# Three shifts in the order of issue of a fused attention and spectral-filter kernel

## The chip, the cores and the metric

The kernel runs on one core of one Trainium2 chip. The metric is the device time of one execution in microseconds. Times inside an execution are counted from the start of the span, which runs from the first to the last instruction of the profile.

The engines go by short names: PE is TensorE (its weight loads are shown as PEld), ACT is ScalarE, DVE is VectorE, POOL is GpSimd, SP is SyncE. Each takes its instructions in a fixed order of its own, and an instruction that waits holds up all that stand behind it on that engine. SP and POOL do little here but issue DMAs, and a row marked SPq or POOLq is such an issue.

## The reference

Two independent computations are put side by side in the output.

```python
# A: 16 query heads share one key head and one value head; S = 2048, D = 448, Dh = 28
q = (x @ wq) split into 16 heads;  k = x @ wk;  v = x @ wv
p = softmax(q k^T * Dh**-0.5);     a = (p v, heads joined) @ wo
# B: a filter in the frequency plane of a 2048 x 448 array
X = rfft2(x);  b = irfft2(X * (w_r + 1j * w_i))
out = concatenate([a, b], axis=-1)
```

## The kernel before

**First stage (about 0 to 69 us).** The queries and, folded into their spare rows, the keys and values are projected into `qraw`. The key and value rows are picked out of `qraw` by small DMAs (`fetch`, line 277) into `kf`: rows 0 to 31 are keys, rows 32 to 63 values. `fetch` takes row groups `ms`; groups 7 to 13 are value rows. The last two value groups, 12 and 13, for the last 512 positions, come out of the last projection and are fetched at line 479 through POOL. The value rows are then turned by 16 transposes on PE (line 509) and copied to `vs` (line 512). The queries of the first chunk are built at line 469. Each query is kept as two pieces, a high part `qh` and a low part `ql`, in four bands of 32 partitions of one tile, `qf`, for each of four heads; `copy_q` (line 207) writes one band of one head. Bands 2 and 3 are written by DMAs, band 2 by SP and band 3 by POOL (lines 486 and 487). Between these pieces of work the first transform of B is done (`fft1_...`), which stores its result in DRAM (`t1`). In this stage PE's order is the order of the program text, while the other engines' order is chosen by a scheduler; `behind(a, b)` only says that `a` is issued after `b` on their engine, with no wait.

**Main stage (about 69 us to the end).** There are 256 steps: 4 chunks of 512 queries, 4 groups of 4 heads, 16 blocks of 128 keys. A step makes four score products on PE (line 929), each into a PSUM bank of its own; their exponentials on ACT (line 864); and four value products (line 875) into one bank. There are eight banks, six named `s` and two (`sx`, `po`) that come from the first stage; one of the eight collects the value products and seven go round. `PLAN` (line 48) holds the steps in groups, each a string. `-` is a score whose exponential ACT takes straight from the bank. `k` is a score that DVE first copies out of its bank (line 935), with the exponential of a pair of copies made later at line 954. `e` is a score that ACT takes into the same kind of tile (line 940). Letters are units of other work on PE: `A` and `B` the two halves of the filter's middle stage, `W` a quarter or so of an output block (four `W` in a row finish one block of 128 rows), `Z` the filter's last stage. `spread` (line 38) makes the string; its fourth argument, `start`, sets how late the letters stand. Four `W` in a row are a `wo_unit` (line 799) for each of the four head groups.

DVE and ACT run in the order of the program text here. DVE's other work goes through a planner: `put` queues pieces of work with a cost, `passed(work)` moves PE's planned clock on after each product and takes pieces from the queue as long as DVE's planned clock isn't ahead of PE's, and `need` takes pieces until a given one is done. `at(step, f)` runs `f` when a step's scores are all issued.

**The middle stage's input.** `fft2_load(0)` (line 594) reads B's first result back from `t1` into the tile `b` with four DMAs on SP (line 599). `fft2_split(0)` (line 612) puts two pieces in the queue, a rounded copy `bh` (line 617) and the rest, written over `b` (line 618). `fft2_a(0)` (line 620) multiplies both on PE (lines 586 to 588). The first `A` stands in the group of steps 8 to 12, whose string is `-k-k-k-k----------A--`, at step 11.

**An output block's input.** `norm` puts the division and splitting of a head group's attention output in the queue; its last piece (line 772) is followed by small DMAs (`spares`, line 741) that bring some rows to spare partitions of `oh` (by SP, line 746) and `ol` (by POOL, line 749).

Of the kernel before, what the change touches and what calls it, by code (L numbers as in the profile page):

```python
# [20 lines left out]
S, D, H = 2048, 448, 16  # L21
# [16 lines left out]
def spread(n, units, lazy=4, start=0.9, rest=0.85, apart=1.0):  # L38

    late = 8 if lazy > 4 else 4  # L40
    m = 4 * n - late
    out = [(float(i), "-") for i in range(m)]
    out += [(apart * j + 0.5 if j < lazy else m + 0.1 * j, "k" if j < lazy else "e") for j in range(late)]
    out += [(m * (j + start) / (len(units) + rest) - 0.4, u) for j, u in enumerate(units)]
    return "".join(k for _, k in sorted(out)).replace("X", "WWWW").replace("Y", "ZZ")


PLAN = ["eeee"] + ["eeeeF"] + [spread(2, "", 0, 1.05)] + 2 * [spread(2, "", 0)] + [spread(5, "A", 4, 1.6)]
# [5 lines left out]
PLAN += [spread(6, "BAX", 4, 0.9, 0.85, 1.5)] + [spread(5, "BA", 4, 0.9, 0.6)]  # L54
PLAN += [spread(7, "BBX", 5, 0.9, 1.1)] + [spread(7, "ZZ", 8, 0.9, 0.85, 2.0)]
PLAN += [spread(7, "ZZZ", 6, 0.9, 0.48, 2.0)] + [spread(7, "ZZ", 8, 0.9, 0.6, 1.5)]
PLAN += [spread(7, "ZZZ", 6, 0.9, 0.6, 2.0)] + [spread(6, "X", 8, 0.9, 0.6, 2.0)]
PLAN += [spread(7, "X", 8, 0.6, 0.6, 1.5)] + [spread(8, "X", 8, 0.9, 0.6, 1.5)]
PLAN += [spread(7, "X", 8, 0.6, 0.35, 1.5)] + [spread(7, "ZZZ", 8, 0.9, 0.6, 1.5)]
PLAN += [spread(7, "Z", 8, 0.45, 0.6, 2.0)] + [spread(7, "ZZZ", 8, 0.9, 0.97, 2.5)]  # L60
# [12 lines left out]
def kernel(ctx: ExitStack, tc: tile.TileContext, t: dict):  # L73
    nc = tc.nc
# [21 lines left out]
    def behind(ins, other):  # L96

        tc.add_manual_dep(ins.ins, other.ins.name,
                          mybir.DependencyInfo(mybir.DependencyClass.NoSync, mybir.DependencyReason.DATA),
                          reason="order of issue")  # L100
# [65 lines left out]
    def fft1_b(q):  # L166
        return fft1_out(q, fft1_mm(q))
# [39 lines left out]
    def copy_q(i, p, q, src, eng):  # L207

        o, x = q[32 * p:32 * p + 32, i], src[32 * i:32 * i + 32].bitcast(F32)
        if eng is nc.scalar:  # L210
            return eng.activation(o, x, AF.Copy)
        if eng is nc.vector:
            return eng.tensor_copy(o, x)
        return eng.dma_start(o.bitcast(F32), x)

    def build_q(c, g, first=False):
        cs = slice(c * CW, (c + 1) * CW)
        qh = qp.tile([128, CW], F32R, name="qh", bufs=1)
        ql = qp.tile([128, CW], F32R, name="ql", bufs=1)
        qt = ql.bitcast(F32)  # L220
        if (c, g) not in qa:
            qa[c, g] = qp.tile([128, 4, CW], F32R, name="qa")
        q = qa[c, g]

        def split():
            nc.vector.tensor_tensor(ql, qt, qh.bitcast(F32), op=ALU.subtract)
            if first:
                return
            for i in range(4):
                for p, src in enumerate((qh, ql)):  # L230
                    mv = nc.sync.dma_start(q[32 * p:32 * p + 32, i].bitcast(F32), src[32 * i:32 * i + 32].bitcast(F32))
                    behind(mv, stored[-1])
            nc.sync.dma_start(q[64:128].bitcast(F32), q[0:64].bitcast(F32))

        def high():
            if first:
                return nc.scalar.activation(qh, qt, AF.Copy)
            return nc.vector.tensor_copy(qh, qt)

        ops = [(540, lambda: nc.vector.tensor_scalar(qt, qraw[:, g, cs], mask, cvec[:, g, c:c + 1],  # L240
                                                     op0=ALU.mult, op1=ALU.add)),
               (450, high), (710, split)]
        if not first:
            return ops
        for _, op in ops:
            op()
        return q, qh, ql
# [17 lines left out]
    with tc.tile_pool(name="w1", bufs=1) as w1:  # L265
# [11 lines left out]
        def fetch(ms, hs, eng=nc.sync):  # L277

            for m in ms:
                r, o = 32 * (m % 4) + DH, 32 * (m // 7) + 4 * (m % 7)  # L280
                last = eng.dma_start(kf[o:o + 4, hs], qraw[r:r + 4, m // 4, hs])
            return last
# [20 lines left out]
        with tc.tile_pool(name="x1", bufs=2) as x1:  # L303
# [127 lines left out]
            for c in range(1, NC):  # L431
                for g in range(NG):
# [25 lines left out]
                    if n in slots:  # L458
# [3 lines left out]
                        if n == 10:  # L462
# [6 lines left out]
                            qf, qh, ql = build_q(0, 0, True)  # L469
# [6 lines left out]
                            fft1_fold(q + 2, None if q < 3 else 0)  # L476
                        if q:
                            fft1_b(q - 1)
            fetch(range(12, 14), slice(1536, S), nc.gpsimd)


        behind(copy_q(0, 1, qf, ql, nc.scalar), last)
# [1 line left out]
            last = fft1_a_out(6, p, fft1_a_mm(6, p))  # L484
        for i in range(4):
            copy_q(i, 2, qf, qh, nc.sync)
            copy_q(i, 3, qf, ql, nc.gpsimd)
        behind(copy_q(1, 1, qf, ql, nc.scalar), last)
        top = terms(1, NC)
        for ins in fft1_fold(7, 1):  # L490
# [325 lines left out]
    def at(step, f, *a):  # L816
        later.setdefault(max(step, 0), []).append((f, a))
# [8 lines left out]
    where, total = {}, 0  # L826
# [6 lines left out]
        total += n  # L833
    fft2_consts()
    at(1, fft2_load, 0)
    at(where["A"][0] - 1, fft2_split, 0)
    at(where["B"][-1] + 1, fft3_consts)
    for u, step in enumerate(where["A"]):
        if u % 2 == 0 and u < 14:
# [66 lines left out]
    for tokens in PLAN:  # L906
# [10 lines left out]
        for k in tokens:  # L917
# [5 lines left out]
            i, h = divmod(x[kind], 4)  # L923
# [274 lines left out]
```

## Time and profile before

| | us |
|---|---|
| three timed runs | 633.93, 634.25, 634.91 |
| median of them | 634.25 |
| the profiled execution | 633.88 |
| its span | 632.1 |
| PE busy in the span | 626.7 (99%) |
| ACT busy | 547.3 (87%) |
| DVE busy | 440.2 (70%) |
| POOL busy | 61.5 (10%) |

In the rows of the timeline the first number is the start in the span, the second the duration, then engine, line, operation, tiles (out<-in), shape and count. A row can stand for several instructions of a kind in a row (x4). Brackets tell how long the engine was idle before it, and what ended that. Products on PE overlap, so that a start, not an end, tells how PE gets on: scores follow each other every 0.23 us where nothing holds them up.

### The profile page before, as it was taken

Reading aid. Unit: us, or ns where it says so; the run is one execution under the profiler, and the core shown is the slowest. Engines: PE = TensorE matmul, PEld = TensorE weight load, DVE = VectorE, ACT = ScalarE, POOL = GpSimd, SP = SyncE. Lnnn points to the kernel's source line nnn. Section 1 sums busy time; section 2 is a strip of 40 time slices with the busy share of each in tenths; the row PEclk is TensorE's granted clock in tenths of the full one; section 3 lists DMA queues with packets and bytes.
Section 4 is the critical chain, followed back from the end, with each engine's and each line's share of the span. In section 5 each row is a group of like instructions: output and inputs, shape, how many; then the busy total and the mean of one; then the engine's idle time right before and its main releaser. Section 6 shows DMA issues by size and latency. Waiting matters only on the chain. (4 is left out here: it accounts for less than half of the span.)

```text
span 632.1 us, 12164 instructions
## 1 busy us (share of the span) xinstructions
PE 626.7 (99%) x4436; PEld 377.6 (60%) x4436; DVE 440.2 (70%) x792; ACT 547.3 (87%) x985; POOL 61.5 (10%) x118
## 2 busy tenths in 40 slices
PE   9999999999999999999999999999999999999997
PEld 7877645656565655746555665565556565555555
DVE  5999648889998943867766845277687764457753
ACT  5655999999999998988889989999989989989991
POOL 3021401021212110000110100001010100000000
PEclk9999999999999999999999999999999999999999
DMA  8865973456455523226340413034152413030011
GB/s 260 285 175 165 271 161 92 111 147 184 117 153 123 147 58 74 69 64 187 77 108 16 125 36 82 16 83 148 37 127 60 104 51 90 16 82 13 19 31 61
DMA packets 37891, 66.74 MB, mean 106 GB/s; under 512 B 8009, under 2 KB 22746, under 8 KB 36860
## 3 DMA queue, kind: packets, MB, share of 16 engines
q1 hardware_dynamic: 32608, 52.50, 30.2%
q0 software_dynamic: 4640, 12.48, 7.9%
q8 instruction: 36, 0.59, 0.4%
q10 hardware_dynamic: 576, 0.92, 0.4%
q14 instruction: 31, 0.25, 0.1%
HBM read 29.81 MB, written 17.87 MB: 75 GB/s over the span
## 5 line engine op out<-in xcount | busy, mean ns | idle before, releaser
L864 ACT ACTIVATE p<-s 128x512 f32<-128x512 f32 x405 | 221.7, 635 | 26.8 <-PE s L929 26.1
L929 PE MATMUL s<-qa,ka 128*128 128x512 f32 x756 | 227.5, 402 | 0.0
L929 PEld LDWEIGHTS s<-qa,ka 128*128 128x128 f32 x756 | 138.2, 188 | 60.8 <-issue 26.8
L935 DVE COPY k<-s 128x512 f32<-128x512 f32 x122 | 80.1, 685 | 62.8 <-PE s L929 62.4
L875 PE MATMUL s<-p,vs 128*32 128x512 f32 x976 | 121.3, 595 | 0.0
L864 ACT ACTIVATE qraw<-s 128x512 f32<-128x512 f32 x137 | 79.0, 651 | 6.4 <-PE s L929 6.4
L954 ACT ACTIVATE k<-k 128x1024 f32<-128x1024 f32 x80 | 83.4, 1141 | 0.0
L875 PEld LDWEIGHTS s<-p,vs 128*32 128x32 f32 x976 | 29.4, 109 | 64.3 <-issue 59.4
L929 PE MATMUL sx<-qa,ka 128*128 128x512 f32 x137 | 55.2, 403 | 0.0
L929 PE MATMUL po<-qa,ka 128*128 128x512 f32 x131 | 53.0, 405 | 0.0
L864 ACT ACTIVATE p<-po 128x512 f32<-128x512 f32 x75 | 47.9, 639 | 4.5 <-PE po L929 4.2
L875 PE MATMUL s<-qraw,vs 128*32 128x512 f32 x384 | 49.5, 593 | 0.0
L864 ACT ACTIVATE p<-sx 128x512 f32<-128x512 f32 x64 | 41.2, 644 | 3.0 <-PE sx L929 2.9
L749 POOL DMA_DIRECT2D ol<-ol x36 | 18.0, 507 | 227.4 <-DVE ol L772 155.3
L875 PE MATMUL s<-k,vs 128*32 128x512 f32 x304 | 39.7, 594 | 0.0
L929 PEld LDWEIGHTS sx<-qa,ka 128*128 128x128 f32 x137 | 25.8, 188 | 11.0 <-issue 4.2
L929 PEld LDWEIGHTS po<-qa,ka 128*128 128x128 f32 x131 | 24.6, 188 | 11.0 <-issue 5.0
L879 DVE STREAM_TRANSPOSE osb<-s 128x512 f32<-128x512 f32 x13 | 9.3, 716 | 27.7 <-PE s L875 27.6
L875 PEld LDWEIGHTS s<-qraw,vs 128*32 128x32 f32 x384 | 12.0, 110 | 27.3 <-issue 26.1
L935 DVE COPY k<-po 128x512 f32<-128x512 f32 x17 | 11.7, 685 | 21.4 <-PE po L929 21.3
L864 ACT ACTIVATE qraw<-sx 128x512 f32<-128x512 f32 x35 | 22.7, 649 | 2.0 <-PE sx L929 2.0
L935 DVE COPY p<-s 128x512 f32<-128x512 f32 x35 | 23.0, 682 | 0.0
(278 smaller groups left out, 972.7 us busy)
## 6 DMA issues: line engine op xcount, KB each, us to landing
qa<-qa SPq DMA_DIRECT2D x15, 512.0 KB
raw<-xa SPq DMA_DIRECT2D x16, 256.0 KB
xb<-xb SPq DMA_DIRECT2D x8, 512.0 KB
qa<-qh SPq DMA_DIRECT2D x64, 64.0 KB
qa<-ql SPq DMA_DIRECT2D x60, 64.0 KB
t<-bs SPq DMA_DIRECT2D x16, 225.0 KB
wr<-wr POOLq DMA_DIRECT2D x16, 225.0 KB, 4.0
wi<-wi POOLq DMA_DIRECT2D x16, 225.0 KB, 5.4
```

The costliest lines, as they stand in the source:

```text
L749: nc.gpsimd.dma_start(ol[c][o, g].bitcast(F32), ol[c][r, 0].bitcast(F32))
L864: nc.scalar.activation(tiles[-1][:, h % 2], sc, AF.Exp, scale=SCALE)
L875: mm(po[c, g][32 * i:32 * i + 32], vs[:, kc], ps[i // 2][:, i % 2], start=(n == 1), stop=(n == 16))
L879: nc.vector.transpose(o, po[c, g])
L929: begun.append(mm(sc, ka[:, kc * 128:(kc + 1) * 128], qa[c, g][:, h], start=True, stop=True))
L935: nc.vector.tensor_copy(keep[i][h // 2][:, h % 2], sc)
L954: nc.scalar.activation(p, p, AF.Exp, scale=SCALE)
```

## The change

Three places change, and none adds or removes an instruction.

```diff
-PLAN += [spread(7, "ZZZ", 6, 0.9, 0.6, 2.0)] + [spread(6, "X", 8, 0.9, 0.6, 2.0)]
+PLAN += [spread(7, "ZZZ", 6, 0.9, 0.6, 2.0)] + [spread(6, "X", 8, 1.15, 0.6, 2.0)]
...
-            fetch(range(12, 14), slice(1536, S), nc.gpsimd)
+            fetched = fetch(range(12, 14), slice(1536, S), nc.gpsimd)
...
         for i in range(4):
             copy_q(i, 2, qf, qh, nc.sync)
-            copy_q(i, 3, qf, ql, nc.gpsimd)
+            behind(copy_q(i, 3, qf, ql, nc.gpsimd), fetched)
...
-    at(where["A"][0] - 1, fft2_split, 0)
+    at(where["A"][0] - 4, fft2_split, 0)
```

- On POOL the four DMAs of band 3 of the first queries are issued after the two DMAs that fetch the last value rows.
- The split of the filter's first input is put in the planner's queue after step 7 instead of after step 10.
- In the group of steps 137 to 142 the four output units stand later. The string goes from `-k--k--k--k--kWWWW--k--k--k-` to `-k--k--k--k--k--k-WWWW-k--k-`: three `-` and one `k` now stand ahead of them.

## The prediction

> **What bounds the kernel now.** I began with the page's first part, went on to the stages that the three edits touch, and ended with the waits there.
>
> ```profile
> span 632.1 us, 12164 instructions
> PE 626.7 (99%) x4436; PEld 377.6 (60%) x4436; DVE 440.2 (70%) x792; ACT 547.3 (87%) x985; POOL 61.5 (10%) x118
> ```
>
> PE is never without a product for long, so a delay of PE anywhere is paid at the end, unless a later wait absorbs it; a gain must be a place where two starts on PE stand further apart than usual. The first edit's place is the change from the first stage to the second, shown first by POOL's timeline.
>
> ```profile
> 62.81 1.04 POOL L214 DMA_DIRECT2D qa<-ql  x2 [4.01 <-DVE ql L226]
> 63.83 1.02 POOL L281 DMA_DIRECT2D kf<-qraw  x2
> 64.84 1.19 POOL L214 DMA_DIRECT2D qa<-ql  x2
> ```
>
> The DMAs issued in the second and in the third of these stretches, with the us from issue to landing as the last number:
>
> ```profile
> kf<-qraw POOLq DMA_DIRECT2D x2, 8.0 KB, 4.3
> qa<-ql POOLq DMA_DIRECT2D x2, 64.0 KB, 3.9
> ```
>
> The value transposes, in the window of their first part, and PE's timeline from their last part on:
>
> ```profile
> L509 PE MATMUL s<-ident,kf x12: 220/222/243, 67.5 to 68.2; 32*128 32x32 f32 x12
> L509 PEldq EVENT_SEMAPHORE  x1: 901/901/901, 67.6 to 67.6; - x1
> ```
>
> ```profile
> 68.51 0.40 PE L509 MATMUL s<-ident,kf 32*128 32x32 f32 x4
> 68.84 1.44 PE L929 MATMUL s<-qa,ka 128*128 128x512 f32 x5
> ```
>
> The reader is to see that PE's queue stood 0.9 us, from 67.6 to 68.5, at a semaphore before the last four transposes, while the last value rows, issued at 63.83 and 64.3, landed 4.3 us later.
>
> The second edit's place is shown by the timelines of DVE, PE and ACT, one fence each.
>
> ```profile
> 85.51 1.29 DVE L935 COPY k<-s 128x512 f32<-128x512 f32 x2 [10.68 <-PE s L929]
> 86.72 0.68 DVE L935 COPY k<-sx 128x512 f32<-128x512 f32 x1
> 87.31 0.68 DVE L935 COPY k<-s 128x512 f32<-128x512 f32 x1
> 87.91 0.39 DVE L617 CAST bh<-b 128x450 fp32r<-128x450 f32 x1
> 88.33 0.63 DVE L618 TENSOR_TENSOR b<-b,bh 128x450 fp32r<-128x450 f32 x1
> ```
>
> ```profile
> 86.37 1.32 PE L929 MATMUL s<-qa,ka 128*128 128x512 f32 x5
> 87.53 0.42 PE L929 MATMUL sx<-qa,ka 128*128 128x512 f32 x1
> ...
> 89.35 0.44 PE L586 MATMUL s<-bh,g1h 128*128 128x450 f32 x1
> ```
>
> ```profile
> 87.11 2.14 ACT L864 ACTIVATE p<-s 128x512 f32<-128x512 f32 x4
> 89.02 0.72 ACT L864 ACTIVATE p<-sx 128x512 f32<-128x512 f32 x1
> ...
> 92.36 0.81 ACT L864 ACTIVATE p<-po 128x512 f32<-128x512 f32 x1
> ...
> 95.74 0.60 ACT L864 ACTIVATE p<-s 128x512 f32<-128x512 f32 x1 [0.54 <-PE s L929]
> ```
>
> Then SP's issues, the longest wait of its queue between 81 and 90, the semaphore instructions ahead of the split, and two stretches (busy us of PE, PEld, DVE, ACT and POOL with their counts, PE's clock, the DMA engines' share, GB/s):
>
> ```profile
> 77.91 1.93 SPq L599 DMA_DIRECT2D b<-t  x4
> ...
> 85.19 0.51 SPq L231 DMA_DIRECT2D qa<-ql  x1
> ```
>
> ```profile
> SPq L231 <- DMA b<-t: 1.9, 1, 1.9
> ```
>
> ```profile
> L617 DVEq EVENT_SEMAPHORE  x2: 21/35/49, 86.8 to 86.9; - x2
> ```
>
> ```profile
> 74.80:85.50 10.70, 10.70 (x70) 5.12 (x69) 0.04 (x1) 10.70 (x23) 2.63 (x5) 1.00 1.00 235
> 85.50:90.70 5.20, 5.17 (x21) 3.36 (x19) 3.83 (x7) 5.20 (x12) 0.00 (x0) 1.00 0.67 152
> ```
>
> To be seen: DVE is idle for 10.7 us before its copies at 85.51, ACT is busy without a break (10.70 of 10.70 us, then 5.20 of 5.20), and the DMA engines are busy all the time before 85.5 (share 1.00). SP's issue at 85.19 had waited 1.9 us for a DMA of `b`, so the first piece of `b` landed about then. At 86.8 the semaphores ahead of the split cost 21 to 49 ns, so by then all four pieces were there.
>
> The third edit's place, in the timelines of PE, ACT and DVE, one fence each:
>
> ```profile
> 364.34 0.37 PE L785 MATMUL s<-woh,oh 128*128 128x448 f32 x1
> ...
> 365.76 0.37 PE L785 MATMUL s<-wol,oh 128*128 128x448 f32 x1
> 366.35 0.44 PE L785 MATMUL s<-woh,oh 128*128 128x448 f32 x1 [0.22 <-DMA oh<-ol]
> ...
> 367.97 0.39 PE L929 MATMUL po<-qa,ka 128*128 128x512 f32 x1
> ```
>
> ```profile
> 363.53 1.12 ACT L864 ACTIVATE p<-s 128x512 f32<-128x512 f32 x2
> ```
>
> ```profile
> 364.54 0.69 DVE L935 COPY p<-s 128x512 f32<-128x512 f32 x1
> ```
>
> **The change part by part.** *POOL's order.* Nothing is added; two issues of the last value rows (1.02 us) go ahead of two of the queries' low parts (1.04 us), which take their slots. The fetch reads a projection and the copies read `ql`; by the program the fetch has no later input than the copies, so I let it issue at 62.81, 1.02 us sooner, and land about as much sooner. The wait before the last transposes then ends by 67.5, and PE gains what lies between 68.51 and the normal place of the thirteenth transpose. Twelve began in 67.5 to 68.2, some 0.065 apart, so the thirteenth would have begun at about 68.28: 0.23 us. What is late next: the low parts that are moved back one slot each. Heads 0 and 1 would be issued at 63.83 and 64.3 and land, by 4.3 us for that slot, at 68.1 and 68.6; their scores would start at 68.61 and 68.84 or later. The other two keep their slots (64.84, plus 3.9 is 68.7; then 69.2) and their scores start at 69.1 and 69.3. So it just fits, with 0.1 to 0.5 us to spare. Price: 0 to -0.23 us; the loads for the filter that POOL issues next keep their slots.
>
> *The split, three steps sooner.* By the planner's rules, worked by hand: after step 7 DVE's planned clock lies 512 below PE's, so that the first score of step 8 takes both pieces (400, then 630) at once. On DVE the order becomes `bh`, `b`, then the four copies of 85.51 to 87.31, instead of the copies first. No other instruction of DVE moves. Queued behind the split are therefore four copies that empty PSUM banks, and behind them the scores that use these banks next.
>
> Does the split find its data? It needs all four pieces of `b`. They were issued over 1.93 us from 77.91, some 0.5 apart. The first was there at 85.19 and the last by 86.8; 85.19 plus three times 0.5 is 86.7, all at once would be 85.2. I take 86.4, near the late end because the issues were spread; these are estimates from the rows above. As the DMA engines are busy all through 74.8 to 85.5, I expect no more than part of the first edit's 0.23 us to reach this landing, and take 0.1: 86.3.
>
> Then, in the times of the trace before: `bh` from 86.3, `b` done 1.05 later (87.91 to 88.96), the first copy done 0.60 after that (0.68 less 0.08 of overlap), 87.95. A score follows 0.13 after its bank's copy where it waits for it (the copy of 86.72 ends at 87.40, the score into that bank starts at 87.53), so the score that takes the first copy's bank starts at 88.08. By the planner's order of banks it is the second of the five scores that begin at 86.37, at 86.60. PE is 1.48 us late there. The copies that follow come 0.60 apart against scores 0.46 apart, which costs a further 0.1 that the later waits take up.
>
> What hides it? ACT cannot catch up: it has exponentials back to back from 87.11 to 92.36, one each 0.48 us (four from 87.11 to 89.02), and its first one after the held score comes 1.48 later as well. PE's waits in 88 to 90.5 are for banks that ACT frees, so these shift along. ACT's only slack is the 0.54 us at 95.74, and that is idle time while PE is the later one. So nothing gives the 1.48 us back.
>
> What does the split gain? The filter's product at 89.35 follows the split's end at 88.96, but its bank is emptied by the last of the four exponentials of 87.11, which ends at 89.25. The bank, not the split, sets 89.35. So the gain is 0. Price of this edit with the first: +1.48 us; if `b` were to land at 86.8 it is +1.98, if at 85.2 it is +0.38. The first edit's gain isn't added, because PE waits here for a landing and not for its own earlier work.
>
> The first piece took 85.19 less 77.91, 7.3 us, to land. Beside this, the Trainium skill's page "DMA: Bandwidth & Descriptors", section "Anatomy of one DMA — SWDGE (gpsimd) path", puts a DMA at some 2.0 us and its bytes over 436 GB/s. That is fitted for POOL's path, but by it, as an estimate, a piece of 112.5 KB lands 2.3 us after issue, by 82, this edit costs nothing, and the sum is that of the first rival. The trace does not agree, with DMA engines that are busy throughout.
>
> *The output units, four scores later.* Three `-` and one `k` go ahead. The last third of the units stood at 366.35, 0.59 us after the product at 365.76, where 0.20 is usual (364.34 to 365.76 holds seven of these steps); it waits for a spare-row DMA. Later units lose this wait: 0.39 us and a slow start. But the scores now issued in their place need banks: one takes the bank whose exponential ends at 364.65 (the second of 363.53), against 364.57 at PE's own pace, and the units take the bank whose DVE copy ends at 365.23. I get a start at 365.42, 1.08 us later, instead of 0.93. The units' eleven products at 0.203 take 2.23, so the score of 367.97 comes at 367.65: -0.32 us. Upper end 0 (the DMA's landing shifts too), lower end -0.47. DVE's copy of the output block goes one copy later, and its store on SP too; nobody waits for that.
>
> Sum: +1.48 - 0.32 = +1.16 us. On the profiled execution's 633.88 this is 635.04; that one lies 0.37 below the median of the runs, so I forecast 634.25 + 1.16 = 635.4. It is within 0.2% (1.27 us, about what a measurement of this kernel can tell from no change), near its upper edge.
>
> **The rivals.** *The split finds its data.* If `b` lands by 84.8 in the changed kernel (86.60 less the 1.78 from landing to score), the copies wait for nothing, and the three edits give -0.23 - 0.32 = -0.55 us: 633.7. The change's second edit would then do nothing at all, as the bank sets 89.35. For it: the loads were issued 7 us before, and DVE is idle all that time. Against it: SP's 1.9 us wait ending at 85.19, and the full DMA engines.
>
> *The last piece comes at the late end.* One mechanism, at the same place: every 0.1 us of later landing costs 0.1 us of PE. It decides from 86.4 on, where the sum passes 1.27. At the bound, 86.8, the sum is 1.98 - 0.32 = +1.66: 635.9, slower. For it: the spacing of the issues gives 86.7, and earlier loads put elsewhere could fill the DMA engines sooner. Against it: SP went on issuing at 85.19 and the engines are less full from 85.5 (0.67).
>
> *The moved low parts are late.* If POOL's DMAs in their new slots take 0.5 us longer than 4.3, the first scores wait up to 0.3 us. PE then has less to wait for at 88.08, so that the total stays: 635.4. It would matter only together with the first rival.
>
> **How the numbers follow.** Forecast (landing 85.9 to 86.4, total +0.8 to +1.27): 0.43. Late end (over +1.27): 0.41. Split finds its data, or nearly: 0.13. The rest, 0.03, is for gains over 1.27 us, for which no wait in the rows is large enough. The range goes from the first rival's 633.7 to 636.2, 0.3 beyond the late end's 635.9; the likeliest case alone has 635.0 to 635.5. Faster by over 0.2%: 0.03; within, the forecast and the first rival: 0.56; slower, the late end: 0.41.
>
> **What would show it.** Right: DVE's row for `bh` stands ahead of the four copies and starts at the landing of `b`, near 86.3; a PE row of scores starts some 1.5 us after its forerunner, released by DVE; the wait before the last four transposes is gone or small; the output units have no wait for `oh<-ol`. Wrong: `bh` starts before 85, or scores go on at 0.23 while DVE waits because other banks are free.

## The result and the profile after

The changed kernel takes 635.94 us (median of 13 runs, 634.26 to 638.31), the kernel before 634.23 us in the 13 runs beside it. The ratio is 1.0028, with a 95% interval of 1.0018 to 1.0039: the change makes the kernel slower by 0.28%, 1.7 us. The profiled execution of the changed kernel took 635.16 us, 1.28 more than that of the kernel before.

The first part of the page of the changed kernel:

```profile
span 633.4 us, 12162 instructions
PE 627.1 (99%) x4436; PEld 377.8 (60%) x4436; DVE 440.0 (69%) x792; ACT 547.7 (86%) x985; POOL 61.1 (10%) x118
```

The busy times are those of before within 0.4 us, and the span is 1.3 longer. The loss is time in which PE stands. First, the place of the first edit: POOL's timeline, the waits of the transposes, and PE's timeline from the transposes on.

```profile
62.93 1.00 POOL L281 DMA_DIRECT2D kf<-qraw  x2 [4.01 <-ACT qraw L371]
63.92 2.00 POOL L214 DMA_DIRECT2D qa<-ql  x4
```

```profile
L509 PE MATMUL s<-ident,kf x16: 220/222/243, 67.6 to 68.6; 32*128 32x32 f32 x16
```

```profile
67.78 1.03 PE L509 MATMUL s<-ident,kf 32*128 32x32 f32 x14
68.74 2.24 PE L929 MATMUL s<-qa,ka 128*128 128x512 f32 x8
```

The value rows are issued first, all 16 transposes run in one piece, and the first score starts at 68.74 instead of 68.84, although PE's starts were 0.12 late in this execution until then. Now the place of the second edit, the timelines of DVE, PE and ACT:

```profile
86.34 0.40 DVE L617 CAST bh<-b 128x450 fp32r<-128x450 f32 x1 [11.60 <-DMA b<-t]
86.77 0.63 DVE L618 TENSOR_TENSOR b<-b,bh 128x450 fp32r<-128x450 f32 x1
87.32 1.28 DVE L935 COPY k<-s 128x512 f32<-128x512 f32 x2
88.52 0.68 DVE L935 COPY k<-sx 128x512 f32<-128x512 f32 x1
89.11 0.68 DVE L935 COPY k<-s 128x512 f32<-128x512 f32 x1
```

```profile
86.27 0.40 PE L929 MATMUL s<-qa,ka 128*128 128x512 f32 x1
88.06 1.33 PE L929 MATMUL s<-qa,ka 128*128 128x512 f32 x4 [1.39 <-DVE k L935]
...
90.80 0.44 PE L586 MATMUL s<-bh,g1h 128*128 128x450 f32 x1
```

```profile
86.53 0.66 ACT L864 ACTIVATE p<-po 128x512 f32<-128x512 f32 x1
88.59 2.06 ACT L864 ACTIVATE p<-s 128x512 f32<-128x512 f32 x4 [1.40 <-PE s L929]
```

DVE waits for the DMA of `b` until 86.34; the four copies stand behind it; one score goes at 86.27 and the next, which stood at 86.60 before, at 88.06. PE waits 1.39 us for a copy and ACT 1.40 us for a score. The filter's product, at 89.35 before, is 1.45 late, at 90.80. Last, PE's timeline at the output units:

```profile
366.98 0.37 PE L785 MATMUL s<-woh,oh 128*128 128x448 f32 x1
...
369.00 0.37 PE L785 MATMUL s<-wol,oh 128*128 128x448 f32 x1
369.20 0.40 PE L929 MATMUL po<-qa,ka 128*128 128x512 f32 x1
```

The eleven products stand 0.20 apart with no wait for `oh<-ol`, and the score that stood at 367.97 is now 1.23 late in these rows (369.20).

### The profile page after: what moved, and what is told of

Its sections match the earlier page's. It is cut to its first block, busy times and chain, and to the rows that moved or that the text cites. A ratio compares the mean times of both kernels' runs of the same rounds, so it can differ in the third digit from the quotient of the medians.

```text
span 633.4 us, 12162 instructions
## 1 busy us (share of the span) xinstructions
PE 627.1 (99%) x4436; PEld 377.8 (60%) x4436; DVE 440.0 (69%) x792; ACT 547.7 (86%) x985; POOL 61.1 (10%) x118
## 5 line engine op out<-in xcount | busy, mean ns | idle before, releaser
L864 ACT ACTIVATE p<-s 128x512 f32<-128x512 f32 x416 | 227.1, 635 | 28.8 <-PE s L929 28.0
L929 PE MATMUL s<-qa,ka 128*128 128x512 f32 x766 | 231.1, 403 | 1.4 <-DVE k L935 1.4
L875 PE MATMUL s<-p,vs 128*32 128x512 f32 x896 | 111.8, 595 | 0.0
L875 PEld LDWEIGHTS s<-p,vs 128*32 128x32 f32 x896 | 27.0, 109 | 58.6 <-issue 54.0
L929 PE MATMUL po<-qa,ka 128*128 128x512 f32 x121 | 48.5, 401 | 0.0
L875 PE MATMUL s<-qraw,vs 128*32 128x512 f32 x352 | 45.4, 593 | 0.0
L864 ACT ACTIVATE p<-po 128x512 f32<-128x512 f32 x63 | 40.0, 635 | 2.5 <-PE po L929 2.5
L875 PE MATMUL s<-k,vs 128*32 128x512 f32 x288 | 37.6, 594 | 0.0
L875 PE MATMUL po<-p,vs 128*32 128x512 f32 x248 | 30.0, 594 | 0.0
L929 PEld LDWEIGHTS po<-qa,ka 128*128 128x128 f32 x121 | 22.7, 188 | 8.4 <-issue 2.5
```

The source lines that it names most:

```text
L864: nc.scalar.activation(tiles[-1][:, h % 2], sc, AF.Exp, scale=SCALE)
L875: mm(po[c, g][32 * i:32 * i + 32], vs[:, kc], ps[i // 2][:, i % 2], start=(n == 1), stop=(n == 16))
L929: begun.append(mm(sc, ka[:, kc * 128:(kc + 1) * 128], qa[c, g][:, h], start=True, stop=True))
```

## The experiments

The theory at this point was that of the prediction: DVE stands at the split until the last piece of `b` has landed, and holds the banks of four scores meanwhile (A in the expectations; A1 adds that the landing is late because POOL's loads of `wr` and `wi` are ahead in the DMA engines). Against it stood that the loss comes from elsewhere in the change (B), and that DVE's new order costs by itself, whenever `b` lands (C). Two were added later: that PE's delay stops growing with the landing (D), and that PE's clock falls after a long wait (E).

The kernel before was run again beside the experiments, and each ratio is to the runs beside it. Its medians there were 634.87, 634.69 and 634.66 us (35, 14 and 15 runs, from 633.60 to 636.72).

**The second edit alone.** The kernel before with one line changed.

```diff
-    at(where["A"][0] - 1, fft2_split, 0)
+    at(where["A"][0] - 4, fft2_split, 0)
```

> Before plus the second edit alone (the split three steps sooner). Theory A (DVE stands at the split until the last piece of b lands, and the copies behind it hold PE's banks): all the loss is here and the other two edits only gain 0.3 us, so 636.2 us, about 2.0 over before, the runs spread over 2 us or more because the landing varies, and in the profile bh ahead of the four copies, starting at 86 to 88. Theory B (the loss comes from one of the other two edits, POOL's order or the output units): within 0.3 us of before, 634.2.

Measured: 635.8 us (median of 12), ratio to the kernel before 1.0022 [1.0010, 1.0035]. PE's timeline shows the wait of the changed kernel:

```profile
88.13 1.10 PE L929 MATMUL s<-qa,ka 128*128 128x512 f32 x3 [1.40 <-DVE k L935]
```

One line gives the loss. SP's timeline and SP's waits in this execution:

```profile
82.42 1.76 SPq L599 DMA_DIRECT2D b<-t  x4
```

```profile
SPq L599 <- DMA t<-bs: 4.7, 1, 4.7
```

Here `b` was issued only at 82.42, after 4.7 us of waiting for a store to `t`, and the held score still came within 0.1 us of that of the changed kernel, where the issue was at 78.32 (below). What precedes the landing isn't the same in each execution. SP stood at this place for 4.6 to 5.3 us in four of the twelve profiles of this document (this one, the kernel with other data and the two that load `b` twice), and the first load of `b` was issued at 81.6 to 84.1 there; in the other eight SP stood for 0.9 to 1.4 us, and the issue came at 77.6 to 79.0.

**The other two edits alone.** The changed kernel with that line as before.

```diff
-    at(where["A"][0] - 4, fft2_split, 0)
+    at(where["A"][0] - 1, fft2_split, 0)
```

> The changed kernel with the split put back to its old step; POOL's order and the output units stay changed. Theory A: 0.1 us gained before the last transposes and 0.22 at the output units, 633.9 us, runs within 1 us of each other. Theory B: 635.5 us or more.

Measured: 634.27 us (median of 11, 633.79 to 634.72), ratio 0.9993 [0.9984, 1.0002]. DVE's timeline is the old one, with the copies first:

```profile
85.39 1.29 DVE L935 COPY k<-s 128x512 f32<-128x512 f32 x2 [10.67 <-PE s L929]
...
87.79 0.39 DVE L617 CAST bh<-b 128x450 fp32r<-128x450 f32 x1
```

The two edits lose nothing; a gain of 0.2 us or so, as PE's starts have it, is less than the interval. The split at 87.79 finds its data.

**The new order with data that is there.** The split stands where the change puts it, but reads `qraw` instead of `b` and writes its rest into another tile, so that the filter's first rows are not computed from `b`.

```diff
+        if u == 0:
+            bl = b2["l", 0] = fp.tile([128, 2, DF], F32R, name="bl", tag="cst")
+            old = qraw[:, 3, 0:2 * DF].rearrange("p (n f) -> p n f", n=2)
+            put(("split", 0), [
+                (400, lambda: nc.vector.tensor_copy(bh, old)),
+                (630, lambda: nc.vector.tensor_tensor(bl, old, bh.bitcast(F32), op=ALU.subtract))], True)
+            return
```

> The changed kernel, the split at the early place, but the first of the sixteen splits takes its input from the raw queries, which lie in SBUF long before, and writes its low part to another tile; the filter's first two rows of points are therefore left out of the result. Nothing else moves. Theory A (the landing): DVE finds its data, does the split while it is idle, and the loss is gone: 633.9 us, spread under 1 us, no wait of PE at the second score of step 8's group. Theory C (the order alone costs: two more pieces of work ahead of four copies that empty banks): still 0.8 to 1.3 us over before, 635.0 to 635.5.

Measured: 634.42 us (median of 11), ratio 0.9995 [0.9986, 1.0004]. DVE's timeline, and PE's around the place:

```profile
75.63 0.39 DVE L620 CAST bh<-qraw 128x450 fp32r<-128x450 f32 x1
...
86.30 1.29 DVE L942 COPY k<-s 128x512 f32<-128x512 f32 x2 [9.61 <-PE s L936]
```

```profile
87.15 1.32 PE L936 MATMUL s<-qa,ka 128*128 128x512 f32 x5
...
90.18 0.44 PE L586 MATMUL s<-bh,g1h 128*128 128x450 f32 x1
```

The order by itself costs nothing that the runs can tell. It gains nothing either: with the split done 10 us ahead, the filter's product starts 3.03 us after the five scores (90.18 less 87.15), and in the kernel before it was 2.98 (89.35 less 86.37). The product waits for its bank, as the prediction had it.

**`b` ahead of the other loads.** The changed kernel, with four of the eight loads of `wr` and `wi` that stand ahead of `b` (those for q = 1) issued by SP behind `b` instead of by POOL ahead of it. All bytes are still moved.

```diff
-                ld = nc.gpsimd.dma_start(b2[n, q][64 * r:64 * r + 64], t[n][:, 4 * q:4 * q + 4])
+                eng = nc.sync if q == 1 else nc.gpsimd
+                ld = eng.dma_start(b2[n, q][64 * r:64 * r + 64], t[n][:, 4 * q:4 * q + 4])
```

> The changed kernel with the four filter weight loads of the second quarter (900 KB, issued by POOL from 75 us on) issued by SP behind the loads of b instead. Theory A1 (b lands late because these loads fill the DMA engines ahead of it): the last piece of b lands 2 to 4 us sooner, by 84, and the loss is gone: 633.9 us with a small spread. Theory A2 (b's own stores and reads, or the queries' copies on SP, set the landing): bh still starts at 86 or later and the time stays near 635.9.

Measured: 634.4 us (median of 11, 634.18 to 635.04), ratio 0.9995 [0.9986, 1.0003]. DVE's timeline, and SP's issue of `b` in it and then in the changed kernel:

```profile
83.87 0.40 DVE L618 CAST bh<-b 128x450 fp32r<-128x450 f32 x1 [8.52 <-DMA b<-t]
...
86.02 1.29 DVE L936 COPY k<-s 128x512 f32<-128x512 f32 x2 [1.09 <-PE s L930]
```

```profile
78.90 1.79 SPq L599 DMA_DIRECT2D b<-t  x4
```

```profile
78.32 1.79 SPq L599 DMA_DIRECT2D b<-t  x4
```

Two stretches, first of this kernel and then of the changed one (columns as in the prediction; the last two are the DMA engines' share and GB/s):

```profile
74.80:80.00 5.20, 5.20 (x36) 2.50 (x37) 0.55 (x1) 5.20 (x12) 0.56 (x1) 1.00 0.70 190
80.00:85.00 5.00, 5.00 (x40) 2.18 (x29) 1.02 (x2) 5.00 (x11) 0.00 (x0) 1.00 0.66 179
```

```profile
74.80:80.00 5.20, 5.20 (x37) 2.46 (x40) 0.00 (x0) 5.20 (x12) 2.63 (x5) 1.00 0.98 252
80.00:85.00 5.00, 5.00 (x34) 2.36 (x27) 0.00 (x0) 5.00 (x11) 0.00 (x0) 1.00 1.06 228
```

Issued later than in the changed kernel (78.90 against 78.32), `b` is there 2.5 us sooner (83.87 against 86.34). The DMA engines' share falls from full to 0.7, and the loss is gone. So in the changed kernel `b` was late because of these loads ahead of it.

The same loads with the split where it was before the change:

> The version that the first runs point to: POOL's order and the output units as changed, the second quarter's weight loads behind b, the split at its old late step. Theory A: 634.2 us, level with the kernel without the early split (634.27) and with a spread under 1 us, since b lands long before the split; 0.2 to 0.6 us under before.

Measured: 634.38 us (median of 11), ratio 0.9996 [0.9987, 1.0005], the same as with the early split. With `b` early, it makes no measurable difference where the split stands.

**The landing made later.** The changed kernel with `b` loaded twice, into the same tile.

```diff
-        for r in range(2):
+        for r in (0, 1, 0, 1) if q == 0 else (0, 1):
```

> The changed kernel with the filter's first input loaded twice into the same tile (450 KB more on SP, the same data), so that its last piece lands later. Theory A (every us of later landing is a us of PE): the landing is 2 to 4 us later, bh starts at 88.5 to 90.5, the score behind it 1.72 us after that, and the time is that start plus 548.8: 637.3 to 639.3 us. Theory D (PE's delay saturates, since the other banks and ACT's queue cover the rest): under 636.5. Theory E (the long wait also lowers the granted clock): over 640, with a stretch of clock under 1.0 after 88 us.

Measured: 640.52 us (median of 4, 639.5 to 641.22), ratio 1.0094 [1.0078, 1.0110]. PE's timeline, then three stretches of 3.4 us (the third number from the end is PE's clock):

```profile
86.94 0.40 PE L929 MATMUL s<-qa,ka 128*128 128x512 f32 x1
92.06 1.82 PE L929 MATMUL s<-qa,ka 128*128 128x512 f32 x4 [4.73 <-DVE k L935]
```

```profile
85.63:89.04 3.41, 1.70 (x8) 1.05 (x6) 0.00 (x0) 2.23 (x5) 0.00 (x0) 1.00 0.68 184
89.04:92.46 3.42, 0.40 (x2) 0.30 (x2) 2.08 (x4) 0.00 (x0) 0.00 (x0) 1.00 0.47 125
92.46:95.87 3.41, 3.41 (x10) 2.55 (x9) 1.34 (x3) 3.27 (x7) 0.00 (x0) 0.50 0.69 142
```

`bh` came at 90.35, and the held score 1.71 later, as in the changed kernel (88.06 less 86.34 is 1.72). But after the wait PE's clock was 0.50 for 3.41 us, which the prediction had not foreseen and theory E had. By theory A this execution would have taken 639.15 us (90.35 plus 548.8); it took 640.60.

**The changed kernel twice more,** each a single profiled execution, for how far the landing varies.

> The changed kernel once more, for another profile. Theory A: its time is the start of bh plus 548.8 within 0.4 us, whatever that start is (86 to 89). Theory E: over that by more than 0.5 us where bh starts after 88.

> The changed kernel a third time, for another profile. Theory A: its time is the start of bh plus 548.8 within 0.4 us. Theory E: over that by more than 0.5 us where bh starts after 88.

Measured: 637.53 and 634.75 us. The rows of DVE and PE in the first, two stretches of it, and the same rows in the second:

```profile
86.85 0.39 DVE L617 CAST bh<-b 128x450 fp32r<-128x450 f32 x1 [12.40 <-DMA b<-t]
```

```profile
88.56 1.33 PE L929 MATMUL s<-qa,ka 128*128 128x512 f32 x4 [2.18 <-DVE k L935]
```

```profile
86.94:90.36 3.42, 1.80 (x7) 1.09 (x8) 3.33 (x6) 1.26 (x3) 0.00 (x0) 1.00 0.38 81
90.36:93.77 3.41, 3.41 (x10) 2.60 (x8) 0.36 (x1) 3.41 (x8) 0.00 (x0) 0.50 0.86 209
```

```profile
85.59 0.40 DVE L617 CAST bh<-b 128x450 fp32r<-128x450 f32 x1 [11.12 <-DMA b<-t]
```

```profile
87.30 1.33 PE L929 MATMUL s<-qa,ka 128*128 128x512 f32 x4 [0.91 <-DVE k L935]
```

The same program had `bh` at 86.34, 86.85 and 85.59, and in the first of these two the clock fell as well: a wait of 2.18 us was enough there. Theory A's sum is 634.39 us for the second, 0.36 under the measured time, and 635.65 for the first, 1.88 under it. E had the fall, but only for a `bh` after 88, and here it came with 86.85.

**PE kept busy in the long wait.** `b` loaded twice, and 16 more score products ahead of the held score, into a bank that the next score writes over; no part of the computation is left out.

```diff
+            if begin == 8 and k == "-" and x["-"] == 5:
+                other = min(free, key=lambda x: x[0])[1]
+                for _ in range(16):
+                    mm(other, ka[:, kc * 128:(kc + 1) * 128], qa[c, g][:, h], start=True, stop=True)
             begun.append(mm(sc, ka[:, kc * 128:(kc + 1) * 128], qa[c, g][:, h], start=True, stop=True))
```

> The kernel with `b` loaded twice, and 16 score products more just ahead of the held score, into a bank whose exponential has ended and whose result is written over by the next score into it. Nothing is left out, and the fillers do nothing for the result; they start near 87.3 and at about 0.23 us each fill the wait of PE to about 91. Theory E (the clock of 0.5 that followed the long wait comes from PE standing idle): no stretch of about 3.4 us at 0.5 after 88 us, the held score still starts 1.7 us after `bh`, and the time is the start of `bh` plus 548.8, some 1.3 us less than that of the kernel with `b` loaded twice: about 639.2. Rival (the clock falls for another reason, or its fall costs nothing because ACT sets the pace there): 640.5 or more.

Measured: 638.37 us (median of 6, 637.94 to 642.03), ratio 1.0075 [1.0050, 1.0101]. PE's timeline, and two stretches from the fillers on:

```profile
86.69 3.82 PE L932 MATMUL s<-qa,ka 128*128 128x512 f32 x16
90.35 1.08 PE L933 MATMUL s<-qa,ka 128*128 128x512 f32 x4
```

```profile
87.70:91.10 3.40, 3.40 (x17) 2.75 (x16) 2.90 (x6) 0.33 (x1) 0.00 (x0) 1.00 0.35 79
91.10:94.50 3.40, 3.31 (x17) 2.12 (x19) 1.08 (x2) 3.40 (x8) 0.00 (x0) 1.00 0.57 119
```

The clock stays at 1.00, though ACT had nothing to do for 3.40 us. The held score came 2.18 us after `bh` (88.17), not 1.7 as expected: the fillers ran on for some 0.46 us after the wait would have ended. The medians can't be set against each other, since `bh` came at 88.17 here and at 90.35 in the kernel without the fillers. What can be is the time that is left from the start of the held score to the end of the execution:

| profiled execution | held score at | us | us less start | clock of 0.50 after it |
|---|---|---|---|---|
| changed kernel | 88.06 | 635.16 | 547.10 | no |
| second edit alone | 88.13 | 635.68 | 547.55 | no |
| changed kernel, third execution | 87.30 | 634.75 | 547.45 | no |
| `b` twice, filled | 90.35 | 637.94 | 547.59 | no |
| changed kernel, second execution | 88.56 | 637.53 | 548.97 | yes |
| `b` twice | 92.06 | 640.60 | 548.54 | yes |

The four without a clock of 0.50 have 547.1 to 547.6, the two with it 548.5 to 549.0: it costs some 1.3 us. PE's starts, set side by side with those of the kernel before, place this cost right behind the wait: from the held score to the 100 us mark the four gain 0.04 to 0.17 us on it, and the two lose another 1.08 (`b` twice) and 1.30. The filled kernel had the second longest wait for its copies and is with the four. So a long wait costs PE first the wait itself and can then, if PE stood idle in it, cost slow products. The filled kernel has one profile; it supports PE's idling as the cause, and how long an idle time it takes isn't settled. Of its six runs one, of 642.03 us, has a mean clock of 0.997, as the two executions with a fall have; no profile shows that run.

**Two copies ahead of the split.** The changed kernel, where DVE makes two of the four copies, then the split, then the other two.

```diff
-    at(where["A"][0] - 4, fft2_split, 0)
...
+            if begin == 8 and k == "k" and x["k"] == 2:
+                fft2_split(0)
+                need(("split", 0))
```

> The changed kernel, its split put on DVE behind the first two of the four copies and ahead of the other two. Theory (what counts is the first bank that is held, by way of ACT, which then has no score to work on; ACT has about 2 us of scores in hand when the third bank is held): the scores 9.0 and 9.1 start within 0.3 us of the kernel before, the third copy ends near 89.0 instead of 87.4, its exponential starts about 0.5 late instead of 1.5, and the time is 634.5 to 635.0. Rival (a score that is held counts in full, whichever of the four it is): 1.5 us late at the third score, 635.4 to 635.9, as the changed kernel.

Measured: 634.3 us (median of 10, 633.52 to 635.43), ratio 0.9995 [0.9983, 1.0008]. DVE's and ACT's timelines:

```profile
85.31 1.29 DVE L937 COPY k<-s 128x512 f32<-128x512 f32 x2 [10.67 <-PE s L931]
86.52 0.39 DVE L617 CAST bh<-b 128x450 fp32r<-128x450 f32 x1
...
87.48 0.69 DVE L937 COPY k<-sx 128x512 f32<-128x512 f32 x1
```

```profile
86.91 2.14 ACT L863 ACTIVATE p<-s 128x512 f32<-128x512 f32 x4
88.82 0.72 ACT L863 ACTIVATE p<-po 128x512 f32<-128x512 f32 x1
```

The third copy comes 0.76 later than in the kernel before (87.48 against 86.72, in an execution that was 0.20 ahead at that point), and PE's third and fourth held scores start up to 0.31 later than before. ACT runs on from 86.91 without a break, and the filter's product starts at 89.24, 0.11 ahead of before. Here a late bank is paid only when ACT runs out of scores. The exponentials were to be 0.5 late and are not late at all, so even this expectation was too high. In this execution `b` was there when DVE came to the split (86.52, right behind the second copy), so the profile shows the cost of the order and not that of a late landing; that the ten runs stay under 635.5 speaks for a small one.

None of these kernels is faster than the kernel before by more than its interval.

## Why the prediction was right or wrong

The forecast was 635.4 us, the measured median is 635.94: in the range, but 1.7 us over the kernel before, which is the rival of the late end ("over +1.27") and not the forecast's +1.16.

*POOL's order: right in size, and worth nothing here.* 0.23 us was priced; set side by side with the kernel before, PE's starts gain 0.23 from the transposes to the 86 us mark in each of the ten profiles with this edit, and in that of the second edit alone they lose 0.16. In the changed kernel it vanishes in the wait for `b`, as the prediction said. The low parts that were moved back were in time, so the third rival did not occur.

*The split: mechanism right, step by step.* Landing near 86.3 (86.34 for `bh`), copies behind it, the held score at 88.08 (88.06), +1.48 (+1.45 at the filter's product), ACT without means to catch up, and no gain by the earlier split, since the bank sets the product: each is in the rows, and the kernel with other data shows the last. The split-finds-its-data rival, with the estimate of 2.3 us for a piece by the Trainium skill's page "DMA: Bandwidth & Descriptors", is refuted: from the last issue, an estimated 79.7 (four issues over 1.79 us from 78.32), to `bh` at 86.34 it took some 6.6 us. With the four loads of `wr` and `wi` behind `b`, the same measure is 3.6 (83.87 less an estimated 80.2), nearer to that page's rule.

*The step that failed is the landing as a fixed time* ("I take 86.4, near the late end", then 86.3, with 86.8 as the bound). It fits the one profiled execution to 0.04 us, which is luck, for the landing is not the same in each: `bh` at 85.59, 86.34 and 86.85 in three executions of this program, and 634.26 to 638.31 in its 13 runs, while the kernel with `b` early stays in 634.18 to 635.04. (The kernel before is not that steady either: 633.79 to 634.91 in the 13 runs beside the change, 633.60 to 636.72 in the 64 beside the experiments. No profile shows what its slower runs waited for.) In the kernel before, the split stood behind the copies at 87.91, which hid a landing anywhere up to then; its trace showed one landing, and I took the bounds on that one for the bounds on all. By the table a median run would have its held score at 635.94 less 547.4, 88.5 us, and so the landing near 86.8, the rival's late end. A sooner landing with the clock's 1.3 us is not what it was: 3.41 us at 0.50 take 0.003 off the mean clock of a run, which was 0.997 in both executions with a fall and 0.998 or more in the other profiles, and the median run has 1.000.

*What was missing is the clock.* The prediction priced a wait of PE at its length. In two of the profiled executions it cost 1.3 us more. It is no part of the median: by the mean clocks (0.997 or less) such a fall came in one of the 13 runs of the changed kernel, the slowest, and in the three slowest of the 12 with the second edit alone. Nor does it belong to the early split alone, since four of the 64 runs of the kernel before, of 636.1 to 636.7 us, have 0.996 or 0.997.

*The output units: right direction, and nearly all of it lost again.* -0.32 us was priced. PE's lag behind the kernel before goes from 1.45 ahead of the units to 1.24 behind them: -0.21. Their first product comes 1.19 later than the earlier place of the units (366.98 less 364.34, less 1.45), where 1.08 was worked out. Then 0.18 is given back at 382 to 384 us, where scores wait (0.16 and 0.17 in the kernels without the early split and with two copies first), which the prediction did not have: the banks go round in another order there. In PE's timeline of the changed kernel

```profile
383.38 1.27 PE L929 MATMUL s<-qa,ka 128*128 128x512 f32 x4
```

four scores take 1.27 us, where three of 0.23 and the last one's 0.40 make 1.09. That the order of the banks is the cause was read from the trace and not tried. What remains, some 0.04 us, can't be told in the times.

## What to carry to other kernels

- An instruction that waits for a late input holds up all that stands behind it on its engine, here four copies. Ahead of work that frees the banks of the critical engine, put only what has data with a margin over the worst landing; the later place had hidden every landing up to 87.9 us at no cost.
- A bound taken from one profiled execution is the bound of that execution. For a transfer that shares full DMA engines, take the spread from several, or clear the way for it.
- Price a wait of PE by what ACT has left to do, and allow for a fall of the clock behind a wait of 2 us or more (some 1.3 us here, where it came).

## What the runs showed of the hardware

*The clock after a wait.* With 7 products (1.80 us busy) in the 3.42 us before, the granted clock was 0.50 for 3.41 us (the changed kernel's second execution); with 2 products (0.40 us busy) likewise (`b` twice). In the changed kernel's profiled execution, whose wait was 1.39 us, it stayed at 1.00 throughout, the stretch with the end of the wait and the next one included:

```profile
87.55:90.97 3.42, 2.92 (x11) 1.85 (x12) 2.24 (x4) 2.38 (x5) 0.00 (x0) 1.00 0.74 153
90.97:94.40 3.43, 3.43 (x29) 1.44 (x32) 2.56 (x4) 3.43 (x8) 0.00 (x0) 1.00 0.51 135
```

The busy time of such a stretch alone doesn't decide: with `b` loaded twice the first one had 8 products and 1.70 us busy, less than the 1.80 above, and the clock of the next was still 1.00. The Trainium skill's page "TensorE: Matmul & The Clock Gate", section "HAM oscillation — how this bites in real kernels", gives as rule of thumb no idle gap of over some 3.4 us. The 0.50 and the 3.4 us agree with the rows; the gap does not: the fall came after a wait of 2.18 us, with PE working again for 1.8 us before it.

*The landing.* The last piece of `b`, of 112.5 KB, was there some 3.6 us after its issue with the engines at a share of 0.7, and some 6.6 us after with them full. With the second edit alone, where it was issued last at an estimated 83.7 and the share was 0.57 from 80 to 85 us, it was 2.7 us (`bh` at 86.42). The same program varied by 1.3 us in three profiles (`bh` 85.59 to 86.85), of which up to 0.9 us is the time of the last issue (78.94, 79.67 and 79.84 in the traces) and the rest lies behind it (6.65, 6.67 and 7.01 us). Why SP's wait for the store to `t` is 4.6 us or more in some executions and 0.9 to 1.4 in others was not found.
